# An attention, MLP and mixer kernel: block 0 of the first MLP in twos, two score steps moved up, one lower word moved to SBUF

## The chip, the cores and the metric

The kernel runs on one core of one Trainium2 chip. The metric is device time in microseconds (us) of one execution, the median of several runs.

## The reference

Three stages in float32. Only the middle one, and the attention that runs beside it, matter here.

```python
# q, k, v: (4, 8, 576, 64); windowed causal attention, window 64
scores = q @ k.T / sqrt(64), masked;  attn = softmax(scores);  x = attn @ v     # -> (4, 576, 512)
# first MLP, channels 512 -> 2048 -> 512
xn = (x - mean) / sqrt(var + 1e-6) * g_ln
x = x + relu(xn @ w_ch1) @ w_ch2
# second block: a token mixer and a second channel MLP, 512 -> 1536 -> 512
```

## The kernel before

The 2304 rows of x are 18 tiles of 128 rows. The first MLP goes over them in five blocks of 3, 3, 4, 4 and 4 tiles (`BLOCKS`). While one block is in the MLP, the attention of later tiles is put between its matmuls. The order of all work on every engine is the order in which the program issues it (`tc.manual_schedule()`); each engine works its queue in that order, and the framework adds the waits between engines.

One block of the MLP (`mlp_block`, `mm1`, `mm2`) walks over 16 chunks of 128 hidden channels. Every matrix operand is split into a high and a low part, so a product is three passes. For chunk f these steps are named here and below:

- **up(f)**: 12 matmuls at line 410 into a bank of PSUM (`ps_h`, two banks), then relu on ScalarE (line 414, the high part) and a VectorE step (line 422, the low part) into `hreg`.
- **down(f)**: 9 matmuls (3 tiles by 3 passes) at line 428 that add to the block's three accumulators. It follows `LAG = 2` chunks behind up(f). With `pairs` set, the loop lets up(f) and up(f+1) run one behind the other, and then down(f-2) and down(f-1), always after an odd chunk. Before, this holds for block 1 (`i == 1`) alone. Both blocks 0 and 1 have 3 tiles, so their matmuls have the same widths.
- The lists `hooks[f]` run behind up(f) and before the downs of that step; `hooks[f - 0.5]` runs inside `mm1`, behind up(f)'s matmuls and ahead of its relu.

Block 0 carries two further streams.

**Weights.** The weights arrive as 64-bit words, 512 KB for one chunk of one of the two matrices, and are made float32 on the chip. `todo` is the order: before, (2,0), (0,1), (3,0), (1,1), (4,0), (2,1) and so on, where (f,0) is what up(f) reads and (f,1) what down(f) reads. `wnarrow(2)`, from `hooks[f - 0.5]`, is four VectorE instructions at lines 140 and 141, and frees two raw buffers, whose next loads it issues on SyncE's queue (five raw buffers in all). It is called **narrow(f)** here. By default the lower word goes into a bank of PSUM (tag `l`, one bank) between the two instructions of a weight. `wsplit` in `hooks[f]` then makes the high part on ScalarE (line 123) and the low part on GpSimd (line 124), and shrinks the next two raw weights on ScalarE (line 131), for which the next narrow waits. The last narrowing, for down(14) and down(15), stands at the end of `hooks[14]`, because chunks 14 and 15 have none of their own.

**Attention of tiles 3, 4 and 5** (`LEAN`). A tile has two halves, u = 2t and 2t+1. **scores(t)** (`att_S`, 32 matmuls at line 208) fills two banks, one for each half; the matmuls of the two halves alternate. VectorE then masks them (8 instructions with as many short ones, line 221) and ScalarE takes 8 exponentials (line 229). **turn(u)** (line 244) is 4 transposes of a half and a copy on ScalarE; **PV(u)** (line 313) is 16 matmuls, and one VectorE instruction that reads the result out of PSUM (line 319). scores, turn and PV all take their banks from the one pool `ps_a`, which has two:

```python
    ps_a = ctx.enter_context(tc.tile_pool(name="ps_a", bufs=2, space=bass.MemoryType.PSUM))
              ps_a.tile(wide, F32, tag="a", name=f"s{2 * t + hh}") for hh in range(2)]
        p_ = ps_a.tile([P, NH, P], F32, tag="a", name=f"pt{u}")
        pool, tag = ((ps_h, "h") if t >= BLOCKS[3][0] else (ps_l, "l")) if len(halves) == 2 else (ps_a, "a")
```

Before, the steps of the chunks are: scores(3) at 1; turn(6) at 3; turn(7), PV(6) at 4; PV(7) at 5; scores(4) at 6; turn(8) at 7; turn(9), PV(8) at 8; PV(9) at 9; scores(5) at 10; turn(10) at 11; turn(11), PV(10) at 12; PV(11) at 13; scores(6) at 14; then at 15 the transposes of block 1's input (`tr3`, line 356, two banks of `ps_a` and the one with tag `l`). PV(7) and PV(9) are followed by a row statistic on VectorE and by the load of the next tile's v; scores(t) is followed by the loads of the next tile's q and k, all on SyncE's queue.

Of the kernel before, what the change touches and what calls it, by code (L numbers as in the profile page):

```python
# [14 lines left out]
ALU = mybir.AluOpType  # L15
AX = mybir.AxisListType

P = 128
B, H, S, D = 4, 8, 576, 64
DM = 512  # L20
KD = DM // P
# [5 lines left out]
TPB = 3  # L27
# [20 lines left out]
WARM = 10  # L48


LEAN = ((1, 3, 4), (1, 4, 5), (6, 7, 8), (6, 8, 9), (10, 11, 12), (10, 12, 13))


LAG = 2
# [20 lines left out]
def mixer_kernel(ctx, tc, qT, kT, v, g, wa1, wa2, tok1, tok2, wb1, wb2, out):  # L75
    nc = tc.nc
    FA = wa1.shape[0] // P
# [55 lines left out]
    def narrow(pairs, low=None):  # L133

        for d, r in pairs:
            w = r.rearrange("p (n two) -> p n two", two=2)
            low = d if low is None else low
            nc.vector.tensor_scalar(out=low, in0=w[:, :, 0], scalar1=29, scalar2=None, op0=ALU.logical_shift_right)  # L140
            nc.vector.scalar_tensor_tensor(out=d, in0=w[:, :, 1], scalar=3, in1=low,  # L141
                                           op0=ALU.logical_shift_left, op1=ALU.bitwise_or)
        return [d.bitcast(F32) for d, _ in pairs]

# [216 lines left out]
    xnt = None  # L361
# [39 lines left out]
    def mm1(ws, f, src, i, before, t_):  # L401
        h_ = ps_h.tile([P, src[0].shape[2]], F32, tag="h", name=f"ha_{i}_{f}")
        w = ws[f]
        n = 0
        passes = [(c, a, b) for c in range(KD) for a, b in PASSES]
        if i == 0 and f < LAG:

            passes.sort(key=lambda x: x[1])
        for c, a, b in passes:
            nc.tensor.matmul(h_, lhsT=w[:, a, c * P:(c + 1) * P], rhs=src[c][:, b], start=n == 0, stop=n == 3 * KD - 1)  # L410
            n += 1
        for fn in before:
            fn()
        nc.scalar.activation(out=t_[0], in_=h_, func=AF.Relu)  # L414
        low_h(t_, h_)
        return t_

    def places(n):
        return [hreg[:, k * n:(k + 1) * n] for k in range(6 * N4 // n)]
# [5 lines left out]
    def mm2(ws, f, first, last, t_, acc):  # L425
        for j in range(len(acc)):
            for n, (a, b) in enumerate(PASSES):
                nc.tensor.matmul(acc[j], lhsT=t_[a][:, j * P:(j + 1) * P], rhs=ws[f][:, 2 + b],  # L428
                                 start=f == first and n == 0, stop=f == last and n == 2)

    def mlp_block(i, ws, F, src, hooks, after_last_mm1, pairs, parts):

        acc = [(ps_acc if j < TPB else ps_l).tile([P, DM], F32, tag="acc" if j < TPB else "l", name=f"acca_{i}_{j}")
               for j in range(BLOCKS[i][1])]
        made, due = [], 0
        for f in range(F):
            made.append(mm1(ws, f, src, i, hooks.get(f - 0.5, ()), [x[f % len(x)] for x in parts]))
            for fn in hooks.get(f, ()):
                fn()
            while due <= f - LAG and (f % 2 == 1 or not pairs):  # L440
                mm2(ws, due, 0, F - 1, made[due], acc)
                due += 1
        after_last_mm1()
        for f in range(due, F):
            mm2(ws, f, 0, F - 1, made[f], acc)
            for fn in hooks.get(f + LAG, ()):
                fn()
        return acc

    W = {}  # L450
    ALLP = slice(0, P)
    with tc.manual_schedule():
# [31 lines left out]
        nc.scalar.activation(out=warm, in_=mhalf, func=AF.Exp)  # L484


        todo = [(f, 0) for f in range(LAG)] + [x for f in range(FA) for x in ((f + LAG, 0), (f, 1)) if x[0] < FA]
        place_of = {x: k for k, x in enumerate(todo)}
        ready, raws = [], {}

        def wload(n=1):
            for f, i in todo[:n]:
                raws[f, i] = RAWS[place_of[f, i] % len(RAWS)]
                nc.sync.dma_start(out=raws[f, i], in_=(wa1, wa2)[i][f * P:(f + 1) * P, :].bitcast(U32))
                ready.append((f, i))
            del todo[:n]
# [10 lines left out]
        def wpairs(n):  # L507
            wshrink(n)
            tmps.append(tmps.pop(0))
            tmp = tmps[-1].bitcast(U32)  # L510
            return [(tmp[:, k], raws.pop(x)) for k, x in enumerate(ready[:n])]

        def wnarrow(n=1, psum=True):
            low = ps_l.tile([P, DM], U32, tag="l", name="low") if psum else None
            narrowed.extend((f, i, w) for (f, i), w in zip(ready[:n], narrow(wpairs(n), low)))
            del ready[:n]
            wload(n)
# [32 lines left out]
        for op in FIRST.split():  # L550
            if op[0] == "E" and xnt is None:
                xnf = xnp.tile([P, 8 * N4], F32R, tag="xn", name="xnt")
                xnt = xnf[:, 0:8 * N].rearrange("p (c b n) -> p c b n", c=KD, b=2)
                xn4 = xnf.rearrange("p (c b n) -> p c b n", c=KD, b=2)
# [78 lines left out]
        def piece_narrow(x):  # L633
            n = piece_width(x)
            narrow([(piece_tmp(x, n).bitcast(U32), piece_raw(x)[:, 0:2 * n].bitcast(U32))])
# [88 lines left out]
        def b_narrow():  # L724
            b_shrink()
            _, q, k, raw = ready_b.pop(0)
            if not words:
                words.extend(ps_a.tile([P, DM], U32, tag="a", name=f"word{n}") for n in range(2))
            w_ = reg[:, 6 + 2 * (q % 2)].bitcast(U32) if k else words[0]
            wtmp.setdefault(q, []).extend(narrow([(w_, raw)], words[1]))  # L730
            rawb.append(raw)
            b_load()
# [31 lines left out]
        for i in range(NBLOCKS):  # L764
            hooks = {f: [] for f in range(FA + 2)}
            if i < NBLOCKS - 1:
# [12 lines left out]
                for k in range(2 * TPB if lean else 0):  # L779
# [11 lines left out]
                    u, t = u0 + k, (u0 + k) // 2  # L791
                    fs, ft, fv = LEAN[k]
                    if k % 2 == 0:
# [76 lines left out]
            if i == 0:  # L870
                later_s += [narrows.pop(), narrows.pop()]
                for f in range(FA):
                    if f < FA - 2:
                        hooks[f - 0.5] = [lambda: wnarrow(2)]
                    n = 1 if f in [x[1] for x in LEAN] else 0
                    hooks[f] = hooks[f][:n] + [wsplit] + hooks[f][n:]
                hooks[FA - 2].append(lambda: wnarrow(2))
            if i == 1:
                narrows[:] = [reg[:, 1]] + [lns[:, k] for k in range(4)]
            if i == NBLOCKS - 1:  # L880
                del narrows[0]
            base, nt = BLOCKS[i]
            x_, m = places(nt * P), 4 if i == 1 else 3
            acc = mlp_block(i, W, FA, [(xn4 if nt > TPB else xnt)[:, c] for c in range(KD)], hooks, after, i == 1, (x_[0:m], x_[m:2 * m]))
            for j in range(nt):
                t = base + j
                nc.vector.scalar_tensor_tensor(out=xt[t], in0=acc[j], scalar=mv.pop(t)[:, 1:2], in1=xt[t],
                                               op0=ALU.mult, op1=ALU.add)
# [80 lines left out]
        for op in MIXING.split():  # L969
            k = int(op[1:])  # L970
# [6 lines left out]
        x_ = places(N)  # L977
# [83 lines left out]
        acc = None  # L1061
        for p in range(PAIRS):
            old = acc
            for q in range(HALF):
# [41 lines left out]
                if p < PAIRS - 1:  # L1106
                    if q == 0:
                        ux = qkv.rearrange("p a b n -> p (a b n)").rearrange("p (i c n) -> p i c n", i=2, n=N)
                        per = (6, 7, 7, 6, 6, 0)
                        todo = [(i, k) for i in range(2) for k in range(16)]  # L1110
# [15 lines left out]
                if q == 1:  # L1126
                    acc = []
# [8 lines left out]
        x_ = xt[last + 2][:, half:]  # L1136
# [50 lines left out]
```

## Time and profile before

| | |
|---|---|
| median of 3 runs | 800.63 us (800.58 to 800.71) |
| profiled execution, its own time | 800.34 us |
| its span, first to last instruction | 798.5 us |
| mean granted TensorE clock | 0.999 of full speed |
| busy: PE (TensorE matmul) | 790.0 us, 99% |
| busy: DVE (VectorE) | 499.6 us, 63% |
| busy: ACT (ScalarE) | 329.2 us, 41% |
| busy: POOL (GpSimd) | 174.1 us, 22% |

Block 0 runs from 23.1 us to 106.6 us of the span. The profile counts a matmul as busy from its start to a modelled end, and matmuls overlap; the distance between the starts of two groups of the timeline tells how long the first one kept the engine. In a row of the timeline the columns are the start, the time to the group's end (both us), the engine, the line, the operation, what is written and read, and how many instructions; in brackets stands the idle time before it and what ended that.

### The profile page before, as it was taken

The page shows a single profiled execution, that of the slowest core. Times are in us where ns is not written, and L with a number is a line of the kernel's source. Part 1 is how long each engine was busy: PE and PEld are TensorE (multiplying, and loading weights), DVE is VectorE, ACT ScalarE, POOL GpSimd, SP SyncE. Part 2 cuts the span into 40 slices and gives each one's busy share as a digit, 9 for nine tenths or more (in the row PEclk, how much of TensorE's full clock was granted, in tenths as well). Part 3 has the DMA queues.
Part 4 walks back from the last instruction along what each step waited for, and adds up shares of the span by engine and source line. Part 5 has one row for each costly group of instructions (what it writes and reads, how often), then busy time and mean ns, then how long its engine had stood idle before and what let it go on. Part 6 is the DMA issues. An engine that isn't in the chain of part 4 may idle for free.

```text
span 798.5 us, 12558 instructions
## 1 busy us (share of the span) xinstructions
PE 790.0 (99%) x4722; PEld 678.5 (85%) x4722; DVE 499.6 (63%) x1162; ACT 329.2 (41%) x810; POOL 174.1 (22%) x178
## 2 busy tenths in 40 slices
PE   8999999999999999999999999999999999999998
PEld 6788888888888888888888887889888988988997
DVE  6898667997677765957656137775576544642223
ACT  6887644351433423232445334433453222522221
POOL 4655412010010100000234724301342100410010
PEclk9999999999999999999999999999999999999999
DMA  9788333330313212010387306335640643245202
GB/s 332 257 293 277 122 120 106 113 112 21 98 55 114 86 60 68 18 62 0 132 294 305 113 27 251 105 120 193 237 163 28 238 150 128 92 140 215 94 0 80
DMA packets 33196, 108.16 MB, mean 135 GB/s; under 512 B 3824, under 2 KB 5360, under 8 KB 29936
## 3 DMA queue, kind: packets, MB, share of 16 engines
q1 hardware_dynamic: 32992, 107.10, 38.7%
q8 instruction: 37, 0.61, 0.3%
q10 hardware_dynamic: 144, 0.26, 0.1%
q14 instruction: 23, 0.19, 0.1%
HBM read 86.64 MB, written 20.19 MB: 134 GB/s over the span
## 4 chain that ended last, share of the span: by engine, by line
PE 95%; DVE 2%; ACT 1%; POOL 0%; issue 0%; DVEq 0%; ACTq 0%
PE acca L428 25%; PE ha L410 24%; PE accb L992 17%; PE prod L983 16%; PE th L905 3%; PE td L921 3%; PE o L313 2%; PE s L208 2%; PE accb L1143 1%; PE pt L244 1%; PE td L916 0%; ACT reg L229 0%; DVE reg L141 0%; DVE xnt L375 0%; DVE low L140 0%
## 5 line engine op out<-in xcount | busy, mean ns | idle before, releaser
L410 PE MATMUL ha<-xnt,wa 128*128 128x512 f32 (+1 forms) x960 | 209.8, 369 | 0.8 <-POOL wa L124 0.5
L428 PE MATMUL acca<-wa,hreg 128*128 128x512 f32 x864 | 210.1, 393 | 0.0
L410 PEld LDWEIGHTS ha<-xnt,wa 128*128 128x128 f32 x960 | 175.5, 188 | 26.5 <-DVE xnt L375 1.1
L428 PEld LDWEIGHTS acca<-wa,hreg 128*128 128x128 f32 x864 | 160.2, 188 | 34.9 <-issue 2.2
L992 PE MATMUL accb<-w,hreg 128*128 128x512 f32 x612 | 142.2, 390 | 0.0
L992 PEld LDWEIGHTS accb<-w,hreg 128*128 128x128 f32 x612 | 114.7, 188 | 23.2
L414 ACT ACTIVATE hreg<-ha 128x512 fp32r<-128x512 f32 (+1 forms) x80 | 44.2, 553 | 178.5 <-PE ha L410 178.4
L422 DVE SCALAR_TENSOR_TENSOR hreg<-ha,hreg 128x512 fp32r<-128x512 f32 (+1 forms) x80 | 50.8, 635 | 89.8 <-ACT hreg L414 89.1
L276 DVE STREAM_TRANSPOSE reg<-reg 32x256 f32<-32x256 f32 x176 | 76.7, 436 | 2.5
L1000 POOL TENSOR_TENSOR reg<-reg 128x384 f32<-128x384 f32 x18 | 18.4, 1024 | 210.0 <-ACT reg L997 210.0
L422 DVE SCALAR_TENSOR_TENSOR hreg<-reg,hreg 128x384 fp32r<-128x384 f32 x54 | 32.9, 610 | 46.1 <-ACT hreg L1003 45.9
L997 ACT ACTIVATE reg<-prod 128x384 f32<-128x384 f32 x72 | 35.4, 492 | 62.9 <-PE prod L983 60.5
L983 PE MATMUL prod<-xm,w1b 128*128 128x384 f32 x324 | 59.6, 335 | 0.1
L1003 ACT ACTIVATE hreg<-reg 128x384 fp32r<-128x384 f32 x54 | 28.1, 525 | 71.8 <-PE accb L992 71.8
L983 PEld LDWEIGHTS prod<-xm,w1b 128*128 128x128 f32 x324 | 56.4, 188 | 0.8 <-ACT reg L997 0.6
L229 ACT ACTIVATE reg<-reg,mx 128x128 f32<-128x128 f32 x120 | 46.5, 389 | 21.7 <-DVE mx L221 21.7
L1000 DVE TENSOR_TENSOR reg<-prod,reg 128x384 f32<-128x384 f32 x36 | 20.0, 557 | 56.5 <-PE prod L983 56.4
L340 POOL TENSOR_SCALAR mv<-mv 128x1 f32<-128x1 f32 x13 | 2.5, 196 | 198.5 <-ACT reg L339 198.4
L391 DVE STREAM_TRANSPOSE reg<-reg 32x256 f32<-32x256 f32 x96 | 41.8, 435 | 4.6 <-ACT reg L339 3.3
L983 PE MATMUL prod<-xm,w1a 128*128 128x384 f32 x216 | 41.3, 338 | 0.0
L983 PEld LDWEIGHTS prod<-xm,w1a 128*128 128x128 f32 x216 | 37.7, 188 | 1.1 <-DVE reg L1000 0.5
L383 DVE STREAM_TRANSPOSE reg<-xs 32x384 f32<-32x384 f32 x64 | 36.4, 569 | 1.5
(159 smaller groups left out, 941.4 us busy)
## 6 DMA issues: line engine op xcount, KB each, us to landing
xs<-in_wa SPq DMA_DIRECT2D x32, 512.0 KB, 4.5
w1b<-kept SPq DMA_DIRECT2D x16, 1024.0 KB, 7.0
w1a<-kept SPq DMA_DIRECT2D x16, 768.0 KB, 4.8
reg<-in_v SPq DMA_DIRECT2D x28, 256.0 KB, 3.1
reg<-in_wb SPq DMA_DIRECT2D x14, 512.0 KB, 4.3
kept<-w1b SPq DMA_DIRECT2D x6, 1024.0 KB, 8.8
kept<-w1a SPq DMA_DIRECT2D x6, 768.0 KB, 6.5
more<-in_wb SPq DMA_DIRECT2D x8, 512.0 KB, 3.7
```

What stands on the lines that cost most here:

```text
L229: nc.scalar.activation(out=f_[:, h], in_=f_[:, h], func=AF.Exp, scale=-1.0, bias=mx[:, h], accum_out=sm[:, h])
L276: nc.vector.transpose(out=s_[32 * b:32 * b + 32, :, 32 * a:32 * a + 32], in_=f_[32 * a:32 * a + 32, :, 32 * b:32 * b + 32])
L383: nc.vector.transpose(out=d_[:, :, :, 32 * a:32 * a + 32], in_=s_[:, :, :, 32 * b:32 * b + 32])
L391: nc.vector.transpose(out=d_[:, :, :, 32 * a:32 * a + 32], in_=s_[:, :, :, 32 * b:32 * b + 32])
L410: nc.tensor.matmul(h_, lhsT=w[:, a, c * P:(c + 1) * P], rhs=src[c][:, b], start=n == 0, stop=n == 3 * KD - 1)
L414: nc.scalar.activation(out=t_[0], in_=h_, func=AF.Relu)
L422: nc.vector.scalar_tensor_tensor(out=t_[1], in0=src, scalar=0.0, in1=t_[0].bitcast(F32), op0=ALU.max, op1=ALU.subtract)
L428: nc.tensor.matmul(acc[j], lhsT=t_[a][:, j * P:(j + 1) * P], rhs=ws[f][:, 2 + b], start=f == first and n == 0, stop=f == last and n == 2)
L983: nc.tensor.matmul(dst, lhsT=w_[:, a, c * P:(c + 1) * P], rhs=xm[m][:, c, b], start=first and n == 0, stop=n == 5, skip_group_check=True)
L992: nc.tensor.matmul(acc[j], lhsT=hx[role][a][:, (j % TPB) * P:(j % TPB + 1) * P], rhs=w2[q][:, k, b], start=q == 0 and role in ("21", "12") ...
L997: nc.scalar.activation(out=dst, in_=src, func=AF.Copy)
L1000: eng.tensor_tensor(out=dst, in0=x, in1=y, op=ALU.add)
```

## The change

Four edits, all in block 0 of the first MLP. Block 0 goes in twos as block 1 does, with four places for each part of the hidden values in place of three. The order of the weights becomes (2,0), (3,0), (0,1), (1,1), (4,0), (5,0), (2,1), (3,1) and so on. scores(4) moves from step 6 to step 5 and scores(5) from step 10 to step 9; they are appended behind what stands in those steps, so they come right behind PV(7) and PV(9). The last narrowing keeps its lower words in SBUF, in the place of the result; `narrow` gets a name of its own for that place, so that the second weight of a call uses its own.

```diff
-LEAN = ((1, 3, 4), (1, 4, 5), (6, 7, 8), (6, 8, 9), (10, 11, 12), (10, 12, 13))
+LEAN = ((1, 3, 4), (1, 4, 5), (5, 7, 8), (5, 8, 9), (9, 11, 12), (9, 12, 13))
...
-            low = d if low is None else low
-            nc.vector.tensor_scalar(out=low, in0=w[:, :, 0], scalar1=29, scalar2=None, op0=ALU.logical_shift_right)
-            nc.vector.scalar_tensor_tensor(out=d, in0=w[:, :, 1], scalar=3, in1=low,
+            low_ = d if low is None else low
+            nc.vector.tensor_scalar(out=low_, in0=w[:, :, 0], scalar1=29, scalar2=None, op0=ALU.logical_shift_right)
+            nc.vector.scalar_tensor_tensor(out=d, in0=w[:, :, 1], scalar=3, in1=low_,
...
-        todo = [(f, 0) for f in range(LAG)] + [x for f in range(FA) for x in ((f + LAG, 0), (f, 1)) if x[0] < FA]
+        todo = [(f, 0) for f in range(LAG)]
+        todo += [(f + k, i) for f in range(0, FA, 2) for k, i in ((LAG, 0), (LAG + 1, 0), (0, 1), (1, 1)) if f + k < FA]
...
-                hooks[FA - 2].append(lambda: wnarrow(2))
+                hooks[FA - 2].append(lambda: wnarrow(2, False))
...
-            x_, m = places(nt * P), 4 if i == 1 else 3
-            acc = mlp_block(i, W, FA, [(xn4 if nt > TPB else xnt)[:, c] for c in range(KD)], hooks, after, i == 1, (x_[0:m], x_[m:2 * m]))
+            x_, m = places(nt * P), 4 if nt == TPB else 3
+            acc = mlp_block(i, W, FA, [(xn4 if nt > TPB else xnt)[:, c] for c in range(KD)], hooks, after, nt == TPB, (x_[0:m], x_[m:2 * m]))
```

## Rows read from the trace of the kernel before

**Rows 1.** Waits from 28 to 62 us: who waited for whom, total us, times, longest.
```profile
DVE reg L141 <- ACT xs L131: 1.0, 3, 0.5
...
DVE hreg L422 <- ACT hreg L414: 0.7, 1, 0.7
...
PE ha L410 <- POOL wa L124: 0.5, 1, 0.5
```

**Rows 2.** Timeline of PE, block 0, chunks 2 to 4 and chunk 6.
```profile
31.73 2.24 PE L428 MATMUL acca<-wa,hreg 128*128 128x512 f32 x9
33.81 2.27 PE L410 MATMUL ha<-xnt,wa 128*128 128x384 f32 x12
35.92 0.60 PE L244 MATMUL pt<-ident,reg 128*128 128x128 f32 x4
36.28 2.32 PE L428 MATMUL acca<-wa,hreg 128*128 128x512 f32 x9
38.43 0.51 PE L410 MATMUL ha<-xnt,wa 128*128 128x384 f32 x2
39.44 2.04 PE L410 MATMUL ha<-xnt,wa 128*128 128x384 f32 x10 [0.50 <-POOL wa L124]
41.32 0.60 PE L244 MATMUL pt<-ident,reg 128*128 128x128 f32 x4
41.85 0.69 PE L313 MATMUL o<-reg 128*64 128x64 f32 x16
42.46 2.34 PE L428 MATMUL acca<-wa,hreg 128*128 128x512 f32 x9
...
51.82 1.10 PE L208 MATMUL s<-reg 64*64 64x128 f32 x32
```

**Rows 3.** Timeline of PE, block 1, which already goes in twos.
```profile
127.86 4.38 PE L428 MATMUL acca<-wa,hreg 128*128 128x512 f32 x18
132.07 4.35 PE L410 MATMUL ha<-xnt,wa 128*128 128x384 f32 x24
136.26 4.28 PE L428 MATMUL acca<-wa,hreg 128*128 128x512 f32 x18
```

**Rows 4.** Timeline of ACT: end of the last exponential of half 6.
```profile
34.91 0.20 ACT L229 ACTIVATION_READ_ACCUMULATOR reg<-reg,mx 128x1 f32 x1
```

**Rows 5.** Timeline of DVE, chunk 5: the low part of up(5), PV(7)'s read.
```profile
48.74 0.55 DVE L422 SCALAR_TENSOR_TENSOR hreg<-ha,hreg 128x384 fp32r<-128x384 f32 x1
49.21 0.42 DVE L319 TENSOR_TENSOR xs<-o,sm 128x256 f32<-128x256 f32 x1
```

**Rows 6.** Timeline of PE, the attention ahead of block 0: scores of tile 1.
```profile
8.03 1.09 PE L208 MATMUL s<-kv,q 64*64 64x128 f32 x28 [0.66 <-DVE mx L221]
```

**Rows 7.** Timeline of ACT and DVE, chunks 8 and 9: relu, low part, PV(9)'s read.
```profile
61.96 0.49 ACT L414 ACTIVATE hreg<-ha 128x384 fp32r<-128x384 f32 x1
...
67.91 0.56 DVE L422 SCALAR_TENSOR_TENSOR hreg<-ha,hreg 128x384 fp32r<-128x384 f32 x1 [0.39 <-ACT hreg L414]
...
68.38 0.41 DVE L319 TENSOR_TENSOR xs<-o,sm 128x256 f32<-128x256 f32 x1
```

**Rows 8.** Timeline, a lower word in SBUF; then behind scores(6): down, last mask, last narrowing.
```profile
21.92 0.42 DVE L140 TENSOR_SCALAR xs<-xs 128x512 uint32<-128x512 uint32 x1
...
93.74 2.33 PE L428 MATMUL acca<-wa,hreg 128*128 128x512 f32 x9
...
95.89 0.08 DVE L221 DVE_READ_ACCUMULATOR2_ANT mx<- 128x1 f32 x1
...
98.06 0.69 DVE L141 SCALAR_TENSOR_TENSOR xs<-xs,low 128x512 uint32<-128x512 uint32 x1
```

**Rows 9.** Window sums (PE busy first, granted clock third from the end); groups by line.
```profile
795.40:797.50 2.10, 0.01 (x1) 0.00 (x0) 0.42 (x1) 0.00 (x0) 0.00 (x0) 1.00 0.72 250
797.60:798.50 0.90, 0.00 (x0) 0.00 (x0) 0.00 (x0) 0.00 (x0) 0.00 (x0) 0.50 0.00 0
...
L458 PE MATMUL idle<-hreg 128*128 128x512 f32 x10 | 4.6, 640 | 1.3 <-POOL hreg L455 1.3
```

## The prediction

> **What bounds the kernel now.** I read the waits of block 0 first. Between 28 and 62 us TensorE waits for one thing, 0.50 us for GpSimd's low part of a weight, so it is the bound there; VectorE waits for ScalarE alone, 1.0 and 0.7 us, never for TensorE [rows 1]. The reader should keep the second fact: here VectorE and ScalarE are a chain of their own that runs behind TensorE, and giving them their input earlier doesn't move it. Last I followed the timeline step by step, and asked of each matmul group in the new order when its input and its bank are there. Every us that TensorE loses or gains in block 0 counts in full, as the blocks behind it are bound by the same engine.
>
> **Lengths.** From starts to starts: up(f) 2.11 us (33.81 to 35.92), a single down 2.15 (36.28 to 38.43), a turn ahead of a PV 0.53, a PV 0.61 [rows 2]. In block 1, which goes in twos, two ups take 4.19 and two downs behind scores 4.21 [rows 3].
>
> **Going in twos.** Two downs cost 4.21 in place of 4.30, 0.09 less; two ups 4.19 in place of 4.22. Seven pairs of downs give 0.63 and three unbroken pairs of ups 0.09. The other pairs of ups are split by turns, PVs or scores, which I estimate at up to 0.1 lost each, since TensorE changes groups once more; no row shows one. I take -0.6 in all, between -0.3 and -0.9.
>
> **The wait for GpSimd.** The third matmul of up(4) starts at 39.44, 1.01 behind the first, where two matmuls take 0.35 (a sixth of 2.11): 0.66 lost [rows 2]. The weight (4,0) is still the first of narrow(2) in the new order, so it is ready at the same time. As up(4) will not start before that (next step), the 0.66 is gone. The new order of the weights has no other price that I see: the loads are equal in size and number, (f,1) is still narrowed two steps ahead of its down, and the odd (f,0) come one step sooner.
>
> **turn(6).** In the new order up(3) stands directly behind up(2), which ends at 31.73; 2.08 (4.19 less 2.11) later it is done, at 33.81. turn(6) is next, and needs the exponentials of half 6. They end at 34.91 + 0.20 = 35.11 on ScalarE [rows 4], and nothing ahead of them is moved. So far the downs of step 2 covered that; now TensorE waits, and behind the wait stand down(0), down(1) and up(4). With the last transpose and a signal's way, about 0.25, the downs start at 35.35 in place of 34.17 (33.81 and the turn's 0.36): +1.2, between 0.9 and 1.3. They end at 39.56, so up(4) finds its weight.
>
> **scores(4), moved to step 5.** From 39.56: up(4) 41.67, turn(7) 42.20, PV(6) 42.81, up(5) 45.1 (2.11 and about 0.2 for the two changes of group), PV(7) 45.7. scores(4) is next. It takes both banks of the pool, and they hold PV(6) and PV(7). The second can be written only when VectorE has read PV(7). VectorE's queue has narrow(5) and the low part of up(5) ahead of that read: 48.74, and the read from 49.21 to 49.63 [rows 5]. The change puts nothing new ahead of it and gives the chain nothing sooner that it waits for, so 49.63 stands, and TensorE stands still from 45.7 until then with a signal behind it: +4.0. If the 1.7 us of VectorE's waits for ScalarE fell away it would be 2.3; if TensorE came 0.4 sooner, 4.4. At step 6, where it was, up(6) came between, and scores(4) started at 51.82 with no idle time [rows 2]: that is the cover that the move takes away. That scores can be held in the middle by a read on VectorE is seen ahead of block 0, where 28 matmuls wait 0.66 [rows 6]. Behind the held scores stand down(2), down(3), up(6), and for that last one relu on ScalarE. By these rows the move costs 4.0. The Trainium skill ("Perfetto Trace Analysis", section Optimizing Tensor Performance) says that independent groups of matmuls should go round different banks, so that one is read while the next is made; the sum with scores in banks of their own would have 0 here, and the row of step 6, with its 0, agrees as far as it goes.
>
> Of what scores(4) issues else, the masks go behind that read on VectorE and ahead of narrow(6), and the exponentials ahead of relu(6), which waits for TensorE anyway: TensorE is late, so they are covered, and turn(8) finds them done, two downs and two ups (8.4 us) later. On SyncE's queue the loads of tile 5's q and k come ahead of the next raw weights; these wait for narrow(6), which is behind the masks, so nothing is added.
>
> **scores(5), moved to step 9.** The same again, but VectorE has caught up by then. In the rows relu(8) starts at 61.96 and the read of PV(9) ends at 68.38 + 0.41, 6.83 later, of which 0.39 is waiting for relu(9): 6.44 [rows 7]. Part of narrow(8) lies in it, which now runs under the two downs: one instruction less, about 0.7, is the lower bound, 5.7; I take 6.1. TensorE reaches scores(5) after turn(9) 0.53, PV(8) 0.61, up(9) 2.3 and PV(9) 0.61: 4.05 behind the end of up(8), and relu(8) starts some 0.2 behind that end. 6.1 + 0.2 + 0.1 - 4.05 = +2.4, between 1.9 and 2.7.
>
> **The end of the block, and the lower word.** up(15) now follows scores(6) directly, and `tr3` comes about 2.2 us behind the scores. It needs their banks: the last mask ends at 95.97, 2.23 behind the end of the scores at 93.74 [rows 8]: +0.15 at most. The third part of `tr3` uses the bank in which the last narrowing held its lower words until 98.75, 5.0 behind the scores; in twos that would be a wait of some 2.8, and the edit removes it. In SBUF the first instruction took 0.42 [rows 8], no longer than in PSUM, so that edit costs nothing. The four places of `hreg` cost nothing either.
>
> **Sum.** -0.6 - 0.66 + 1.2 + 4.0 + 2.4 + 0.15 = +6.5.
>
> **The clock.** The 4.0 us are an idle time longer than any in this stretch. The trace shows one fall of the granted clock: it is at full speed until 797.50, TensorE having been idle since 795.4, and at half from 797.60 on [rows 9]. So a gap of 4.0 may well bring it to half speed, the lower of 1.2 and 2.4 GHz, and the gap of 2.4 perhaps. The price of a fall is not less than nothing, and the nearest row is the start, where ten matmuls took 4.6 us [rows 9] in place of ten at 0.23 (4.21 by 18): 2.3 us lost with TensorE working throughout. Part of a slow stretch would lie in the gap itself; I take one fall and 1.3. The Trainium skill ("TensorE: Matmul & The Clock Gate", section HAM oscillation) says that pauses between bursts of matmuls throttle the clock anew each time; by that rule one or two falls are due here, by the undisturbed rows of block 0 none.
>
> The profiled execution took 800.34; with 6.5 and 1.3 it is 808.1. The median of the runs is 0.29 above it: **808.4 us**. The measurement tells 0.2%, 1.6 us, from no change.
>
> **Rivals.**
> 1. The clock stays up: 807.1. For it speaks that it never fell within the span's work, against it that the gaps in it were short: 0.50 and 0.66 us in the rows here [rows 1, 6]. 0.25. Two falls at the full 2.3 would be 811.7: 0.08.
> 2. The chain on VectorE closes up: the read of PV(7) comes 1.7 sooner and that of PV(9) before TensorE gets there. 800.6 + 6.5 - 1.7 - 2.4 = 803.0 without a fall, 804.3 with one. 0.10.
> 3. Not slower: VectorE reads PV(7) about when it is made. At step 5 the read would have to end near 45.7 in place of 49.63, and at step 9 the like; then 1.2 + 0.15 - 0.66 - 0.6 leaves +0.1, 800.7, and with half 6's exponentials in time too 799.5. It decides from the point where the waits ahead of scores(4) and scores(5) are under 1.5 us together. For it: TensorE's order is the only thing that changed; against it: VectorE's queue is not behind TensorE there. 0.10 for no change, 0.03 for a gain above 0.2%, which needs the upper bound of the twos as well.
>
> The forecast itself, one fall or a price near it, has 0.44. Its own range is 807 to 810.5. Slower holds 0.44 + 0.25 + 0.08 + 0.10 = 0.87. The range that leaves out no more than 2 in 10 goes from the second rival with one fall, 804.2, to 811.0.
>
> **What the changed profile would show.** Right: TensorE idle for about 4 us ahead of most matmuls of scores(4) and about 2.4 at scores(5), released by line 319 on VectorE; about 1 us ahead of turn(6), released by an exponential; none at up(4); a granted clock below 1.00 in the windows behind 45 us; two ups 4.2 and two downs 4.2. Wrong: scores(4) starting straight behind PV(7), or the read at line 319 well ahead of 49 us; the sum would then fall to the third rival.

## The result, and the profile after

The changed kernel takes 808.9 us (median of 4 runs, 808.46 to 810.23) where the kernel before takes 800.62 on the same chip: a ratio of 1.0108, 95% interval 1.0096 to 1.012, so 8.3 us slower. The profiled execution is the slowest of the four, 810.23 us with a span of 808.1, and its mean granted clock is 0.994, that of the other three 0.995 to 0.996. In it 0.6 us comes ahead of block 0 (the scores of tile 3 start at 29.10 in place of 28.51). There the changed kernel differs only in the order of the weights' loads, and six of the kernels below, the same up to there, have that start anywhere from 28.50 to 28.91; what sets it is not explained here. The row of before:

```profile
28.51 1.10 PE L208 MATMUL s<-reg 64*64 64x128 f32 x32
```

The waits of TensorE in block 0, 28 to 116 us (who waited for whom, total us, times, longest), against the last of [rows 1]:

```profile
PE s L208 <- DVE xs L319: 5.1, 3, 3.3
PE ha L410 <- DVE hreg L422: 0.4, 1, 0.4
```

The wait for GpSimd is gone. In its place TensorE's scores wait for VectorE's read of a PV. The timeline of TensorE of the changed kernel, to be laid beside [rows 2]:

```profile
29.10 1.10 PE L208 MATMUL s<-reg 64*64 64x128 f32 x32
30.13 2.35 PE L410 MATMUL ha<-xnt,wa 128*128 128x384 f32 x12
32.87 2.38 PE L410 MATMUL ha<-xnt,wa 128*128 128x384 f32 x12 [0.38 <-DVE hreg L422]
35.08 0.97 PE L244 MATMUL pt<-ident,reg 128*128 128x128 f32 x4
35.81 4.37 PE L428 MATMUL acca<-wa,hreg 128*128 128x512 f32 x18
40.02 2.27 PE L410 MATMUL ha<-xnt,wa 128*128 128x384 f32 x12
...
45.55 0.69 PE L313 MATMUL o<-reg 128*64 128x64 f32 x16
46.49 0.44 PE L208 MATMUL s<-reg 64*64 64x128 f32 x4 [0.25 <-DVE xs L319]
50.26 1.97 PE L208 MATMUL s<-reg 64*64 64x128 f32 x28 [3.33 <-DVE xs L319]
52.16 5.82 PE L428 MATMUL acca<-wa,hreg 128*128 128x512 f32 x18
57.81 4.35 PE L410 MATMUL ha<-xnt,wa 128*128 128x384 f32 x24
...
62.35 4.36 PE L428 MATMUL acca<-wa,hreg 128*128 128x512 f32 x18
66.55 2.27 PE L410 MATMUL ha<-xnt,wa 128*128 128x384 f32 x12
...
72.73 0.43 PE L208 MATMUL s<-reg 64*64 64x128 f32 x4
74.66 1.09 PE L208 MATMUL s<-reg 64*64 64x128 f32 x28 [1.50 <-DVE xs L319]
75.69 5.99 PE L428 MATMUL acca<-wa,hreg 128*128 128x512 f32 x18
81.52 4.35 PE L410 MATMUL ha<-xnt,wa 128*128 128x384 f32 x24
```

PV(7) is over at 46.16 (45.55 and its 0.61). Four of the 32 matmuls of scores(4) get through at 46.49, when VectorE has read PV(6), and the other 28 start at 50.26, when it has read PV(7). The same at scores(5): four at 72.73, the rest at 74.66. What they wait for is on VectorE and, ahead of it, on ScalarE. In the timeline of VectorE the first two rows answer to [rows 5], the last two to [rows 7]; the row of ScalarE under it is that of [rows 7] too:

```profile
49.32 0.55 DVE L422 SCALAR_TENSOR_TENSOR hreg<-ha,hreg 128x384 fp32r<-128x384 f32 x1
49.79 0.41 DVE L319 TENSOR_TENSOR xs<-o,sm 128x256 f32<-128x256 f32 x1
...
73.73 0.55 DVE L422 SCALAR_TENSOR_TENSOR hreg<-ha,hreg 128x384 fp32r<-128x384 f32 x1
74.19 0.41 DVE L319 TENSOR_TENSOR xs<-o,sm 128x256 f32<-128x256 f32 x1
```

```profile
68.86 0.49 ACT L414 ACTIVATE hreg<-ha 128x384 fp32r<-128x384 f32 x1 [2.49 <-PE ha L410]
```

The read of PV(7) starts at 49.79, which is 49.20 once the 0.59 of the start is taken off; before it was 49.21. VectorE's chain has moved by 0.01 us. Then the clock, in window sums of the changed kernel (first the window, then PE busy; the granted clock is third from the end):

```profile
45.50:48.40 2.90, 1.17 (x21) 0.74 (x20) 2.73 (x7) 2.64 (x5) 2.28 (x2) 1.00 0.83 261
48.50:55.10 6.60, 4.84 (x35) 3.93 (x36) 5.52 (x24) 4.63 (x19) 3.35 (x4) 0.50 0.89 270
55.30:75.60 20.30, 18.80 (x150) 16.65 (x148) 13.36 (x25) 12.36 (x25) 10.20 (x8) 1.00 0.64 220
75.80:79.00 3.20, 3.20 (x8) 2.52 (x9) 3.03 (x19) 3.02 (x16) 0.83 (x3) 0.50 0.88 305
```

It fell to half speed, 1.2 GHz, in the first wait and again behind the second. The price is read off groups that stand on both sides: the 28 matmuls of scores(4) took 1.90 (50.26 to 52.16), those of scores(5) at full speed 1.03; the downs at 52.16 took 5.65 and those at 75.69 5.83, where the pair at 62.35 took 4.20. That is 0.87 + 1.45 + 1.63 = 3.95 us in this execution.

### The profile page after: what moved, and what is told of

It is laid out like the page before. It is cut to its first block, busy times and chain, and to the rows that moved or that the text cites. A ratio compares the mean times of both kernels' runs of the same rounds, so it can differ in the third digit from the quotient of the medians.

```text
span 808.1 us, 12550 instructions
## 1 busy us (share of the span) xinstructions
PE 795.0 (98%) x4722; PEld 682.4 (84%) x4722; DVE 498.6 (62%) x1162; ACT 329.7 (41%) x810; POOL 174.1 (22%) x178
## 4 chain that ended last, share of the span: by engine, by line
PE 93%; DVE 3%; ACT 2%; issue 0%; POOL 0%; DVEq 0%; ACTq 0%
PE acca L428 25%; PE ha L410 23%; PE accb L993 17%; PE prod L984 16%; PE th L906 3%; PE td L922 3%; PE s L208 2%; PE o L313 2%; PE accb L1144 1%; DVE reg L141 1%; DVE low L140 1%; PE pt L244 1%; PE td L917 0%; ACT xs L131 0%; ACT wa L123 0%
## 5 line engine op out<-in xcount | busy, mean ns | idle before, releaser
L428 PEld LDWEIGHTS acca<-wa,hreg 128*128 128x128 f32 x864 | 162.9, 190 | 35.8 <-issue 2.2
```

## The experiments

The theory was: scores(4) and scores(5) stand straight behind a PV whose bank they need, VectorE reads that PV late for reasons of its own, and the idle time lets the clock fall. Rivals: going in twos costs by itself, or VectorE and ScalarE can't keep up with it, wherever the scores stand; the scores wait for VectorE for another reason than the bank; the falls of the clock cost nothing. All ratios are against runs of the kernel before on the same chip.

**Scores back, twos kept.** The changed kernel with one line undone:

```diff
-LEAN = ((1, 3, 4), (1, 4, 5), (5, 7, 8), (5, 8, 9), (9, 11, 12), (9, 12, 13))
+LEAN = ((1, 3, 4), (1, 4, 5), (6, 7, 8), (6, 8, 9), (10, 11, 12), (10, 12, 13))
```

> The changed kernel with scores(4) and scores(5) back at steps 6 and 10, everything else as changed. Theory (the scores stand straight behind the PV whose bank they need, and VectorE's read of it is late): no wait ahead of the scores and no fall of the clock. A smaller wait comes instead ahead of turn(8) and turn(10), which now follow the scores by one up of 2.2 us, while the exponentials of half 8 ended about 4.0 us behind the scores before: 1.8 each. 800.6 - 0.66 - 0.9 + 1.1 (turn(6)) + 3.6 = 803.7, clock 0.999. Rival (going in twos is what costs, wherever the scores stand): within 1 us of 808.9.

Measured: 802.22 us, ratio 1.0023 (1.0014 to 1.0033), clock 1.0. No scores wait. The smaller wait that was to come instead is in the timeline of TensorE of this kernel, between up(7) and the downs behind turn(8):

```profile
53.05 2.36 PE L410 MATMUL ha<-xnt,wa 128*128 128x384 f32 x12
55.79 1.48 PE L244 MATMUL pt<-ident,reg 128*128 128x128 f32 x4 [0.39 <-ACT reg L229]
57.02 4.36 PE L428 MATMUL acca<-wa,hreg 128*128 128x512 f32 x18
```

up(7) is over 2.19 behind its start, at 55.24, and a turn takes 0.36, so 1.4 are lost before 57.02; at turn(10) it is 0.85. The expectation had 1.8 for each, 1.3 more in all, and 803.7 is 1.5 above the measured time. Without the move the other edits cost 1.8 us, by this wait of the turns and the one at turn(6); the move adds most of the loss.

**Scores sooner, no twos.** The kernel before with the opposite edit of the same line alone.

> The kernel before with the scores moved to steps 5 and 9, nothing else. Theory: the same waits, shorter, as TensorE comes later when it doesn't go in twos. PV(7) ended at 48.06 and VectorE's read of it at 49.63: 1.7 with a signal; PV(9) at 67.89 and its read at 68.79: 1.0. 800.6 + 2.7 = 803.3, and the wait of 0.66 at up(4) stays in it. Rival (the move is harmless without the twos): 800.6.

Measured: 803.03 us, ratio 1.0044 (1.003 to 1.0057). The two waits of its scores in the timeline of TensorE:

```profile
49.64 1.09 PE L208 MATMUL s<-reg 64*64 64x128 f32 x28 [1.80 <-DVE xs L319]
...
70.87 1.09 PE L208 MATMUL s<-reg 64*64 64x128 f32 x28 [0.52 <-DVE xs L319]
```

So the move alone, without any other edit, makes the kernel slower, about as much as the rows of before give (2.6 us, 2.7 expected): VectorE lets go at the same time, and TensorE arrives later than in twos. In the profiled execution the clock stays at full speed through both waits. Two of the five runs took 804.88 and 804.91 us at a mean granted clock of 0.997, the other three 802.72 to 803.03 at 0.999 to 1.0, so in those two the clock seems to have fallen; no profile shows where.

**Gaps filled.** The changed kernel with matmuls that fill the two waits and whose result nobody reads:

```diff
-                    def s1(u=u0 + k):
+                    def s1(u=u0 + k, n=(0, 0, 16, 0, 7, 0)[k]):
                         new_x(u // 2)
+                        fill = ps_h.tile([P, DM], F32, tag="h", name=f"fill{u}") if n else None
+                        for _ in range(n):
+                            nc.tensor.matmul(fill, lhsT=xnf[:, 0:P], rhs=xnf[:, 0:DM], start=True, stop=True)
```

> The changed kernel with 16 matmuls of 512 columns ahead of scores(4) and 7 ahead of scores(5), which write a bank that nobody reads: they fill the two waits (3.6 and 1.6 us) and add nothing to the result. Theory: the waits stay as long as they are, but the granted clock doesn't fall, 0.999, and what the falls cost comes back: 800.6 - 0.66 - 0.9 + 1.1 + 4.0 + 1.8 = 805.9. Rival (the waits are the whole loss, the falls cost nothing): 808.9, or a little more for the added matmuls.

Measured: 805.67 us, ratio 1.0066 (1.0053 to 1.0079), clock 1.0. More work on TensorE, and 3.0 us less loss: 8.28 above before without the filling (808.9 less 800.62), 5.27 with it (805.67 less 800.40). In window sums the granted clock stays at 1.00 where it was 0.50, and in the timeline of TensorE, below it, the downs behind scores(4) take 4.22 again (50.77 to 54.99):

```profile
45.00:56.00 11.00, 11.00 (x89) 9.01 (x89) 9.72 (x32) 8.15 (x26) 5.69 (x6) 1.00 0.90 292
```

```profile
45.66 3.92 PE L785 MATMUL fill<-xnt 128*128 128x512 f32 x16
49.51 1.33 PE L208 MATMUL s<-reg 64*64 64x128 f32 x32
50.77 4.38 PE L428 MATMUL acca<-wa,hreg 128*128 128x512 f32 x18
54.99 1.23 PE L410 MATMUL ha<-xnt,wa 128*128 128x384 f32 x6
```

The waits are no shorter: from the scores of tile 3 to the downs behind scores(4) it is 22.20 us (28.57 to 50.77), and in the changed kernel 23.06 (29.10 to 52.16), of which 0.87 is the slow half of the scores. So the falls are 3.0 of the 8.3 us; the rest is waiting, less what the other edits save.

**The last lower word in PSUM.** The changed kernel with `wnarrow(2)` in place of `wnarrow(2, False)` at the end of `hooks[FA - 2]`.

> The changed kernel with the last narrowing's lower word back in PSUM. Theory: the third part of the transposes of block 1's input waits for the bank until the last narrowing ends, about 5.0 us behind scores(6), where TensorE is there after 2.2 + 0.7: 2.1 us more, 811.0, and the edit is worth that much. Rival (the bank is free in time, or the wait is hidden): 808.9.

Measured: 812.81 us, ratio 1.0151 (1.0137 to 1.0164). The wait is there as worked out, in the waits of TensorE:

```profile
PE s L208 <- DVE xs L319: 5.1, 3, 3.3
PE tpa L356 <- DVE xs L141: 2.1, 1, 2.1
```

The runs are some 4 us above those of the changed kernel, not 2.1, and the granted clock of the runs tells the two parts apart. The profiled execution (810.79 us, clock 0.996) had one fall, in the first wait: the clock is 0.50 from 48.00 to 54.50 and 1.00 from 54.70 to 100.00. It lies 1.9 above the two runs of the changed kernel at 0.996 (808.88 and 808.93; its fourth, 808.46, has 0.995). The other three (812.69 to 813.20) have 0.994, and lie 2.5 to 3.0 above the one run of the changed kernel at 0.994 (810.23). So the wait at line 356 accounts for 2 to 3 us, where 2.1 was worked out, and the rest of the 4 goes with a lower clock, which three of four runs had here and one of four there. Behind which gap it fell in those three, no profile shows.

**Scores behind the downs.** The changed kernel, with scores(4) and scores(5) in their new steps but behind the two downs:

```diff
                 mm2(ws, due, 0, F - 1, made[due], acc)
                 due += 1
+            for fn in hooks.get(f + 0.25, ()):
+                fn()
...
-                        hooks[fs].append(s1)
+                        hooks.setdefault(fs + 0.25, []).append(s1) if k else hooks[fs].append(s1)
```

> The changed kernel with scores(4) and scores(5) still in steps 5 and 9, but issued behind the two downs of that step in place of ahead of them. Theory: the downs (4.2 us) cover VectorE's late read, so no wait ahead of the scores and no fall of the clock, and two ups still lie between the scores and turn(8), so no wait there either. What is left is turn(6) and its up(3) (+1.1), the wait at up(4) gone (-0.66) and the twos (-0.6): 0.2 below the kernel before, no difference that can be told. Rival (VectorE and ScalarE can't keep up with the twos wherever the scores stand): 802 to 804.

Measured: 800.06 us, ratio 0.9996 (0.9987 to 1.0005), clock 1.0. The whole loss is gone, with the twos and the new steps kept. In the timeline of TensorE the downs fill the time until VectorE has read, and scores and turn(8) follow without a break:

```profile
44.99 0.69 PE L313 MATMUL o<-reg 128*64 128x64 f32 x16
45.61 4.37 PE L428 MATMUL acca<-wa,hreg 128*128 128x512 f32 x18
49.91 1.10 PE L208 MATMUL s<-reg 64*64 64x128 f32 x32
50.94 4.44 PE L410 MATMUL ha<-xnt,wa 128*128 128x384 f32 x24
55.22 0.60 PE L244 MATMUL pt<-ident,reg 128*128 128x128 f32 x4
```

**And down(0) ahead of turn(6).** To that, the same cover for the exponentials of half 6:

```diff
+            if i == 0 and f == 3:
+                mm2(ws, 0, 0, F - 1, made[0], acc)
+                due = 1
             for fn in hooks.get(f, ()):
                 fn()
```

> The kernel of the run before, and down(0) ahead of turn(6) in step 3. Theory: the down (2.1 us) covers the end of half 6's exponentials, so the rest of the wait goes too, but for up(3)'s 0.4 for its bank. 0.8 below the kernel before, about 0.1%. Rival (another wait takes its place, at PV(6) or up(4)): as the run before or slower.

Measured: 799.99 us, ratio 0.9995 (0.9986 to 1.0003). The direction fits and the wait at turn(6) is gone; as a time it can't be told from no change. In the profiles the time from scores(3) to block 1 is 77.61 us, 0.17 less than in the run before. What stays is up(3)'s wait for its bank, and it is 0.65 from start to start (up(2) at 29.80, up(3) at 32.56, and an up takes 2.11), not 0.4.

**The order of the weights alone.** The kernel before with the changed `todo`.

> The kernel before with the new order of the weights alone. Theory: nothing, the wait of 0.66 at up(4) stays, as the weight (4,0) comes at the same place: ratio 1.000. Rival (the order brings up(4) its weight sooner): 0.7 faster, and the wait is gone from the profile.

Measured: 800.61 us, ratio 1.0001 (0.9992 to 1.001). Nothing, but not as the theory had it. TensorE's weight loads (PEld) of this kernel:

```profile
PEld acca L428 <- POOL wa L124: 0.6, 1, 0.6
...
PEld ha L410 <- POOL wa L124: 0.3, 1, 0.3
```

The weight (0,1) now comes one step later, so down(0) waits for it, and up(4) waits that much less: from start to start down(0) loses 0.48 and up(4) 0.28, where up(4) alone lost 0.78 before (38.43 to 41.32, less 2.11). The wait for GpSimd's parts stays as long, and the order only chooses who stands in front of them.

**Other banks.** The changed kernel, scores ahead of the downs, but PV(7) and PV(9) in the bank with tag l; narrow(5) and narrow(9) keep their lower words in SBUF so that it is free:

```diff
-        pool, tag = ((ps_h, "h") if t >= BLOCKS[3][0] else (ps_l, "l")) if len(halves) == 2 else (ps_a, "a")
+        pool, tag = ((ps_h, "h") if t >= BLOCKS[3][0] else (ps_l, "l")) if len(halves) == 2 or (t, halves[0]) in ((3, 1), (4, 1)) else (ps_a, "a")
...
-                        hooks[f - 0.5] = [lambda: wnarrow(2)]
+                        hooks[f - 0.5] = [lambda f=f: wnarrow(2, f not in (5, 9))]
```

> The changed kernel, scores ahead of the downs as changed, but PV(7) and PV(9) write the bank with tag l, not the pool that the scores take; so that this bank is free, narrow(5) and narrow(9) keep their lower words in SBUF. Theory (the bank is the cause): both waits ahead of the scores go, but for 0.1 to 0.4 for the read of PV(6), and the clock stays up: between 800.2 and 801.0. Rival (the scores wait for something else of VectorE's queue, not the bank): the waits stay at 4.0 and 1.8, 808 to 809.

Measured: 799.99 us, ratio 0.9997 (0.9988 to 1.0006), clock 1.0. The timelines of TensorE and of VectorE of this kernel:

```profile
45.46 0.69 PE L313 MATMUL o<-reg 128*64 128x64 f32 x16
46.07 1.25 PE L208 MATMUL s<-reg 64*64 64x128 f32 x32
47.25 4.39 PE L428 MATMUL acca<-wa,hreg 128*128 128x512 f32 x18
```

```profile
49.79 0.41 DVE L319 TENSOR_TENSOR xs<-o,sm 128x256 f32<-128x256 f32 x1
```

This is the sharpest of the runs. VectorE reads PV(7) at 49.79, no sooner than in the changed kernel (20.97 behind the scores of tile 3, which start at 28.82, where it was 20.69), and the scores go at 46.07 all the same. So the lower words in SBUF, the other thing that this run changes, did not bring the read forward. It was the bank, and neither VectorE's load nor the place of the scores as such.

**All lower words in SBUF.** The kernel of "down(0) ahead of turn(6)" with `wnarrow(2, False)` in every step of block 0, to get rid of the 0.4 at up(3).

> The kernel with the scores behind the downs and down(0) ahead of turn(6), and the lower words of every narrowing of block 0 in SBUF (0.42 us in place of 0.69 for each of 28 instructions). Theory: VectorE's chain of chunks 0 and 1 gets about 1 us shorter, the low part of up(1) is read sooner, and up(3)'s wait of 0.4 for its bank goes: 0.4 faster than without, 0.9990 of the kernel before. Rival (VectorE's faster form holds up GpSimd's low parts, which then come late at an up or a down): no gain or a loss, with TensorE waiting for line 124.

Measured: 803.76 us, ratio 1.0041 (1.0027 to 1.0055): slower by 3.7 us than without, so the rival's side. Groups of instructions (count, busy us and mean ns, idle before), first of this kernel, then of the one without:

```profile
L124 POOL TENSOR_TENSOR wa<-reg,wa 128x512 fp32r<-128x512 f32 x20 | 29.0, 1469 | 18.3 <-ACT wa L123 14.3 <-DMA reg<-in_v 4.0
L141 DVE SCALAR_TENSOR_TENSOR reg<-xs,reg 128x512 uint32<-128x512 uint32 x19 | 19.1, 1006 | 3.2 <-ACT xs L131 1.1 <-ACT hreg L414 0.5
L140 DVE TENSOR_SCALAR reg<-xs 128x512 uint32<-128x512 uint32 x18 | 11.4, 633 | 0.0
```

```profile
L124 POOL TENSOR_TENSOR wa<-reg,wa 128x512 fp32r<-128x512 f32 x20 | 26.1, 1318 | 17.7 <-ACT wa L123 17.6
L140 DVE TENSOR_SCALAR low<-xs 128x512 uint32<-128x512 uint32 x26 | 17.9, 689 | 0.4
L141 DVE SCALAR_TENSOR_TENSOR reg<-xs,low 128x512 uint32<-128x512 uint32 x19 | 13.1, 688 | 3.1 <-ACT xs L131 1.2
```

Line 140 gains 0.06 us in the mean where 0.27 was counted on, line 141 loses 0.32, and GpSimd's low parts lose 0.15. TensorE does wait, but not for line 124 as that rival had it: it waits 2.6 us for VectorE's low parts of the hidden values (line 422), which stand behind the slower narrowing, and 0.7 at scores.

## Why the prediction was right

**The step that carried it was shown.** scores(4) needs the bank of PV(7), and VectorE reads that bank at a time of its own. The wait was put at 4.0 us and is 4.0: from 46.16 to 50.26, less the 0.13 of the four matmuls in it. The read stayed where it was, to 0.01 us. Three runs change the conditions around it one by one, and the wait goes when the bank is another one, goes when the downs stand in between, and stays, shorter, when only the move is made.

**scores(5) was mis-sized.** 2.4 was forecast, between 1.9 and 2.7; it is 1.8 (72.73 to 74.66, less 0.13). From relu(8) to the end of the read the sum took 6.1; it is 5.74 (68.86 to 74.60). That is the lower bound, but not for its reason: narrow(8) did run wholly under the downs, which took 1.1 off the stretch from relu(8) to its low part, where the bound had 0.7, and the 0.39 of waiting for ScalarE did not go, as VectorE waited 0.63 for it at narrow(9) (line 141, 71.57).

**turn(6):** +1.2 forecast. The downs start 6.71 behind the scores of tile 3 (29.10 to 35.81), where 34.17 less 28.51 is 5.66 without a wait: +1.05. The larger part of it is up(3)'s wait for its bank, which the forecast did not name: up(2) starts at 30.13 and up(3) at 32.87, 0.63 more than an up takes. It hides under the same exponentials, so only what is left of them shows at turn(6).

**The wait for GpSimd** (-0.66, which is 0.78 when the whole of up(4) is counted) is gone, and up(4) starts late enough to find its weight. The claim that the order of the weights has no price holds: in twos down(0) stands in step 3, two steps behind narrow(1), and no wait for line 124 is left. Without the twos it stands in step 2 and waits, as the run with the order alone shows.

**The twos** (-0.6) and the end of the block (+0.15): with the scores behind the downs the time from scores(3) to block 1 is 77.78 us (28.55 to 106.33) in place of 78.05 (28.51 to 106.56), which leaves -0.7 for the twos when +1.05 and -0.66 are taken off, and -0.5 with 0.78. The loss of up to 0.1 for a change of group, for which the prediction names no row, is of that size in the trace of before: an up ahead of a PV takes 2.21 (44.63 to 46.84), 0.10 more than one ahead of a turn. Before `tr3` there is no wait.

**The chain that does not wait.** Of the waits from 28 to 62 us the prediction left out 0.9 of VectorE for ScalarE (61.45) and 1.5 of ScalarE's relu for TensorE, 1.3 of them at relu(6) (51.93). So ScalarE does wait for TensorE from chunk 6 on, as the prediction itself says of relu(6); ahead of the read of PV(7) it is 0.16, and the reading holds there, where the sum needs it.

**The clock was mis-sized.** One fall and 1.3 us were forecast. The price was taken from the start of the span, where ten matmuls took twice their time; the trace gives a granted clock of 1.00 there (0 to 5.60), so that row shows no fall of it, and 1.3 was a guess. The profiled execution had two falls and 3.95, and the filled gaps give 3.0 between medians. The waits and the twos came out lower (5.3 without the falls, 6.5 forecast) and the clock higher (3.0 for 1.3), so the total, 8.3 for 7.8, is closer than its parts: two misses of opposite sign cancel in it, and that is luck. The Trainium skill ("TensorE: Matmul & The Clock Gate", section HAM oscillation) tells of a kernel in which the pauses between bursts of matmuls throttle the clock each time anew. The profile of the changed kernel agrees, with two pauses and two stretches at 0.50; that of the kernel with the last lower word in PSUM does not, with the same two pauses and one stretch.

**The lower word** in SBUF was rightly counted as free, but for a thinner reason than the text gave. It is free at the place where it stands: the two instructions took 0.42 and 0.69 there, with GpSimd idle for 8.31 us until 108.83. The last run shows the price beside a busy GpSimd.

## What to carry to other kernels

When a matmul group is moved up, ask first whose bank it will write and which instruction on which queue must have read it: the reader's own queue sets the time, and it doesn't come sooner because TensorE does. Independent work between the writer of a bank and its next writer (here two downs) cost nothing here and hid the late read; another bank did the same. An idle time of a few us on TensorE can cost more than itself, so compare the time with the gap filled by matmuls that nobody needs before pricing the gap alone. The best of the kernels above, at 799.99 us, can't be told from the one before: the twos gave 0.5 to 0.7 us, which is less than the measurement tells.

## What the runs showed of the hardware

- The granted clock fell in a gap of 4.0 us and behind one of 1.8 in one execution (the changed kernel), and in another (the last lower word in PSUM) only in the first of the same two gaps. In a third (scores sooner, no twos) gaps of 2.1 and 0.8 left it at full speed, though two other runs of that kernel were some 2 us longer at a lower mean clock. All gaps are counted from start to start. So the length of the gap alone does not decide, and no run here shows what does. What a fall took from TensorE's work was 1.6 to 2.3 us.
- VectorE's instructions on two operands in SBUF ran at 1006 ns in the mean beside a busy GpSimd, at 688 with one of them in PSUM, and at 0.69 us with both in SBUF and GpSimd idle (the last narrowing of the changed kernel); GpSimd's went from 1318 to 1469. The Trainium skill ("SBUF — State Buffer", section Who interferes with whom) says that VectorE and GpSimd share one pair of ports, which is locked for one of them at a time: VectorE's two-port form takes the pair for the whole instruction, and an instruction with two inputs in SBUF contends with GpSimd's reads. The means agree with that; which of the two cost more, the run does not tell apart.
